# Block 1's row statistics taken from VectorE to ScalarE and GpSimd, and its normalization placed behind the last copies of block 0

## The chip, the cores and the metric

The kernel runs on one core of one Trainium2 chip. A core has a matrix engine (TensorE, PE in the profile, with its weight loads as PEld), VectorE (DVE), ScalarE (ACT), GpSimd (POOL) and SyncE (SP), which issues most of the DMA transfers. Each engine works through its own list of instructions in order, and an instruction can wait for semaphores that other engines or DMA transfers raise. The metric is the device time of one execution in microseconds (us); smaller is better. Three runs of the kernel before took 1155.17, 1156.48 and 1157.27 us.

## The reference

The reference applies two layers of two parts each to an input of 2048 rows by 512 columns: a long convolution per column (an S4 state space model whose 2048 coefficients are made from A, B, C and dt), and a gated feed-forward net. Each part works on the normalized rows and is added to its input.

```python
def _layernorm(x, axis=-1, eps=1e-5):
    m = jnp.mean(x, axis=axis, keepdims=True)
    v = jnp.var(x, axis=axis, keepdims=True)
    return (x - m) / jnp.sqrt(v + eps)
...
        P = jnp.exp(logdA[:, :, None] * l[None, None, :])
        K = jnp.einsum("dn,dnl,dn->dl", Cc, P, dB).real
...
        Yf = Uf * Kf[None, :, :, :]
...
        y = (lambda x, *d: x.transpose(*d))(y, 0, 2, 1) + u * Dskip[None, None, :]
...
        g = _silu(x @ w_gate)
        u = x @ w_up
        return (g * u) @ w_down
...
    x = A_u
    x = x + _A_ref(_layernorm(x, axis=-1), ...)
    x = x + _B_ref(_layernorm(x, axis=-1), ...)
    x = x + _A_ref(_layernorm(x, axis=-1), ...)
    x = x + _B_ref(_layernorm(x, axis=-1), ...)
```

Uf and Kf are the transforms of the padded rows and coefficients, y the transform of Yf back. The change concerns one of the normalizations: that of rows 512 to 1023 (block 1) ahead of the first convolution. For each row it needs the mean m and 1/sqrt(v + eps); the normalized row is then x times a scale plus a bias of -m times the scale.

## The kernel before

The rows are taken in four blocks of 512, each held as four tiles of 128 rows by 512 columns. The convolution is done with matrix products against constant tables: `direct` (line 290) makes the spectra of a block, four frequency groups q for each of two halves h of the columns, and the copies at line 299 carry each of these eight results from PSUM (pf) to SBUF (u), from where SyncE stores it to DRAM (udr, line 300). Blocks 0 and 1 have their first-layer spectra made early, while the convolution's coefficients are still being built; the later part of the kernel reads them back.

The coefficients are built in eight chunks of 64 columns. For each chunk VectorE builds a table g (`gen_g`, lines 458 to 486) and tables of exponentials times cosines and sines (`gen_e`, lines 444 to 451; line 451 is the last of them). ScalarE makes the exponentials (`gen_exp`, lines 420, 424 and 436), their squares mu (`upper`, line 430), and the cosines and sines (`gen_trig`, lines 406 to 411). TensorE sums over the states in `lags` (lines 496 and 497, into pk), ScalarE copies the result to ks (line 507), SyncE stores it and loads it back in another order as kt (`spread`, lines 514 and 516), VectorE adds the skip term to kt (line 503), TensorE makes kt's spectra pw (line 531), ScalarE copies these (lines 554 and 559), and VectorE adds two parts (line 563). The last doubling of g is added by an accumulating DMA of 1 MB that GpSimd issues (line 476). In between, the largest norms of the weights are summed: GpSimd loads rows of w_down, w_gate and w_up (line 327), ScalarE squares them (line 333), and TensorE sums the squares (nrm, line 336).

From chunk 0's products on, the order of this work is written as a table of times (`plan`), sorted, and issued in that order; the lines that the change touches stand just ahead of that table and are issued in the order in which they are written. For ScalarE, VectorE, TensorE and GpSimd no scheduler reorders them; SyncE's queue is ordered by a scheduler up to the table.

Block 1's rows are the tile x1 (loaded at line 126). Its statistics are taken by `stats` (line 196), the same function as for block 0: VectorE runs one BN_STATS and one BN_AGGR for each of the four row tiles (lines 203 and 204), adds eps (line 205), GpSimd raises to the power -1/2 (line 206), and VectorE makes the bias (line 209). ScalarE applies scale and bias at line 998, between the exponentials of chunk 1 and the last three copies of line 299, and SyncE stores the normalized rows to DRAM (ndr, line 1001). `second` (line 304) loads halves of them back (n1, line 309) for block 1's own `direct`, whose eight parts are spread over the table. The tile kt2, which takes both kt copies, uses x1's buffer.

A second function, `row_stats` (line 212), takes statistics with ScalarE in later stages: an Identity pass with a running sum gives the mean (line 219), a Square pass with a running sum the variance (line 221), a small step adds eps (line 222), GpSimd takes the power (line 223), and VectorE makes the bias (line 224).

Of the kernel before, what the change touches and what calls it, by code (L numbers as in the profile page):

```python
# [13 lines left out]
BF16 = mybir.dt.bfloat16  # L14
I32 = mybir.dt.int32
AF = mybir.ActivationFunctionType
OP = mybir.AluOpType
# [4 lines left out]
L, D, F = 2048, 512, 1376  # L22
P = 128
# [4 lines left out]
HD = D // 2  # L28
# [46 lines left out]
def kernel(ctx, tc, x, a_re, a_im, b_re, b_im, c_re, c_im, log_dt, d_skip,  # L75
                           w_gate, w_up, w_down, c_ef, c_ei, c_ek, c_am, c_eh, c_eih, out):
    nc = tc.nc
    V, A, G, PE = nc.vector, nc.scalar, nc.gpsimd, nc.tensor
# [9 lines left out]
    def tl(shape, name, tag, dt=F32):  # L88
        return sb.tile(shape, dt, name=name, tag=tag, bufs=BUFS[tag])
# [35 lines left out]
    x1 = tl([P, 4, D], "x1", "xf")  # L125
# [9 lines left out]
    mhalf = sb.tile([P, 4], F32, name="mhalf")  # L135
    G.memset(mhalf, -0.5)
    epst = sb.tile([P, 2], F32, name="epst")
# [13 lines left out]
    ndr = dram.tile([2, 2, P, 2, HD], F32, name="ndr")  # L151
# [44 lines left out]
    def stats(src, rows, scale, tag="stats", then=None):  # L196

        st = tl([P, 4, 6], "st", tag)
        mv = tl([P, 4, 2], "mv", tag)
        rs = tl([P, 8], "rs", tag)  # L200
        nb = rs[:, 4:]
        for r in range(rows):
            V.bn_stats(st[:, r], src[:, r])
            V.bn_aggr(mv[:, r], st[:, r])
        V.tensor_scalar(rs[:, :rows], mv[:, :rows, 1], EPS, 1.0 / scale ** 2, OP.add, OP.mult)
        G.tensor_tensor(rs[:, :rows], rs[:, :rows], mhalf[:, :rows], OP.pow)
        if then:
            then()
        V.scalar_tensor_tensor(nb[:, :rows], mv[:, :rows, 0], -1.0, rs[:, :rows], OP.mult, OP.mult)
        return rs, nb  # L210
# [174 lines left out]
    def gen_turns(ch, ts):  # L385

        re, im, mu, xz, mz = ts
        cs = slice(ch * DC, (ch + 1) * DC)
        V.tensor_tensor(xz[:, 1].bitcast(I32), th[:, cs].bitcast(I32).unsqueeze(1).to_broadcast([P, 5, DC]),
                        am.unsqueeze(2).to_broadcast([P, 5, DC]), OP.logical_shift_left)  # L390
        yield
        tu = im[:, 33:65].bitcast(I32)
        V.tensor_tensor(tu[:, 0:2], th32[:, cs].bitcast(I32).unsqueeze(1).to_broadcast([P, 2, DC]),
                        am[:, 0:2].unsqueeze(2).to_broadcast([P, 2, DC]), OP.logical_shift_left)
        yield
        for n in (2, 4, 8, 16):
            V.tensor_tensor(tu[:, n:2 * n], tu[:, 0:n], tu[:, n - 1:n].to_broadcast([P, n, DC]), OP.add)
            yield
        G.memset(im[:, 32], 0.0)
        yield  # L400

    def gen_trig(ts):


        re, im, mu, xz, mz = ts
        A.activation(xz[:, 2], xz[:, 1].bitcast(I32), AF.Sin, scale=-TWO_PI / TURN)
        for c, s in ((xz[:, 0], xz[:, 1]), (re[:, 33:65], im[:, 33:65])):
            turns = s.bitcast(I32)
            A.activation(c, turns, AF.Abs)
            A.activation(s, turns, AF.Sin, scale=TWO_PI / TURN)  # L410
            A.activation(c, c, AF.Sin, scale=-TWO_PI / TURN, bias=hpi)
            yield
# [26 lines left out]
    def gen_e(ts):  # L439


        re, im, mu = ts[:3]
        half = [[t.rearrange("p a (g h d) -> p a g h d", g=4, h=2)[:, :, :, o] for t in (re, mu)] for o in range(2)]
        V.tensor_tensor(im[:, :32], im[:, 64:32:-1], re[:, :32], OP.mult)
        yield
        V.tensor_tensor(re[:, :32], re[:, 64:32:-1], re[:, :32], OP.mult)
        yield
        V.scalar_tensor_tensor(im[:, 33:64], im[:, 31:0:-1], -1.0, mu[:, 1:], OP.mult, OP.mult)
        yield
        for r, u in half:  # L450
            V.tensor_tensor(r[:, 33:64], r[:, 31:0:-1], u[:, 1:], OP.mult)
            yield
# [176 lines left out]
    def take(it, n):  # L629
        for _ in range(n):  # L630
            next(it, None)
# [321 lines left out]
    with tc.manual_schedule(engines={mybir.EngineType.Activation, mybir.EngineType.DVE, mybir.EngineType.PE, mybir.EngineType.Pool}):  # L953
# [3 lines left out]
        def turns():  # L957
            V.tensor_tensor(rho, rho, dt, OP.mult)
            take(first, 1)
            take(ex, 14)  # L960
            take(others, 1)
            take(first, 1)
            take(gen_turns(0, ts[0]), 7)
        ft = tl([P, 2, 2, D], "ft", "ga")
        first, others = turn_units(ft, 0, DC), turn_units(ft, DC, D)
        stats_x = stats(xe, 4, 1.0, then=lambda: (turns(), take(others, 1)))
# [10 lines left out]
        gg = gen_g(0, ts[0], gs[0])  # L977
        ge, tn = gen_e(ts[0]), gen_turns(1, ts[1])
# [2 lines left out]
        upper(ts[0])  # L981
        take(fw[0], 1)
        take(tn, 7)
        stats_x = stats(x1, 4, 1.0, then=lambda: (take(gg, 1), take(ge, 1)))
        tr = gen_trig(ts[1])
        take(tr, 1)
        take(fw[1], 1)
# [6 lines left out]
        take(ex, 14)  # L994
        take(fw[4], 1)
        take(ex, 13)
        for c in range(4):
            A.activation(x1[:, c], x1[:, c], AF.Identity, scale=stats_x[0][:, c:c + 1], bias=stats_x[1][:, c:c + 1])
        for h in range(2):
            for cp in range(2):  # L1000
                nc.sync.dma_start(ndr[h, cp], x1[:, 2 * cp:2 * cp + 2, h * HD:(h + 1) * HD])
        for g in (gg, ge, gg, ge, ge):
            take(g, 1)
        for f in fw[5:]:
            take(f, 1)
        kt2 = tl([P, 2, 4, 16, 16], "kt2", "xf")
        sec = [(h, q) for h in range(2) for q in QORD]
        plan = []
# [87 lines left out]
        for i in range(NCH - 1):  # L1096
# [6 lines left out]
            for k, t0, t1, t2, t3 in ((0, -13.0, 0.25, 13.9, 22.3), (1, 0.3, 14.5, 17.45, 22.9),  # L1103
                                      (2, 15.0, 26.5, 28.05, 36.0)):
                n = ((3, 3, 0), (3, 3, 0), (3, 3, 0), (3, 2, 0), (3, 2, 0), (3, 3, 0), (3, 3, 3))[i][k]
                if i == NCH - 2 and k == 2:
                    t0, t1, t2, t3 = 15.0, 20.0, 24.0, 27.0
# [11 lines left out]
        c, kts, tail = NCH - 1, (kt2[:, 0], kt2[:, 1]), {}  # L1119
# [151 lines left out]
```

## Time and profile before

| | |
|---|---|
| median of three runs | 1156.48 us (1155.17 to 1157.27) |
| the profiled execution's own time | 1156.48 us |
| its span in the profile | 1154.7 us |
| granted TensorE clock, mean | 0.991 |
| BN_STATS of x1 | first at 28.29 us, four of 0.67 us |
| scale and bias of x1 (line 998) | 49.62 us, four passes, 2.92 us |
| first stores of ndr (line 1001) | 51.15 us |
| block 1's first product (pf<-n, line 296) | 64.19 us |

The profile is one execution on the chip. A row of the timeline gives its start from the span's start, the time it took, the engine, the line, the operation, and what it writes and reads; x4 after it means that four such instructions follow each other. In square brackets stand the idle time of the engine ahead of it and what ended that time. In groups by line the figures behind the bar are the total, the mean of one in ns, and the idle time. A row of the DMA view ends with the size of one transfer and the median time from issue to landing. In a table by stretch the busy time of each engine is given; instructions of one engine can overlap by a little, so that rows of the timeline start about 0.1 us before the one ahead has ended.

### The profile page before, as it was taken

How to read it: one execution, taken by the hardware profiler on the slowest of the kernel's cores; microseconds unless marked ns; L12 is line 12 of the kernel's file. 1: busy time of each engine (PE TensorE's matmuls, PEld its weight loads, DVE VectorE, ACT ScalarE, POOL GpSimd, SP SyncE). 2: the span in 40 equal slices, each digit the busy share in tenths (PEclk: the TensorE clock that was granted, in tenths of full speed). 3: DMA queues.
4: the chain of work that ended last, by engine and by line, in shares of the span. 5: the costliest groups of instructions: out<-in, count | busy, mean ns of one | idle time of the engine just before them, and what ended most of it. 6: DMA issues, size and time to landing. Idle time of an engine off the chain costs nothing.

```text
span 1154.7 us, 24400 instructions
## 1 busy us (share of the span) xinstructions
PE 1100.2 (95%) x9942; PEld 877.6 (76%) x9942; DVE 998.7 (86%) x1585; ACT 599.1 (52%) x1198; POOL 109.5 (9%) x163
## 2 busy tenths in 40 slices
PE   2989999998889999999999999999999999999998
PEld 1878888887776868686868687877778686876875
DVE  8999999988889899999899999989994999973211
ACT  6989889734553453567453534555434352334211
POOL 0112222210000010011010001111000100000000
PEclk9989999999899999999999999999999999999999
DMA  5367777867473446332253454343444145312000
GB/s 209 128 165 165 161 185 170 193 186 244 164 240 110 129 139 207 111 102 74 89 153 124 133 156 150 107 120 105 147 121 140 50 130 160 97 37 48 14 24 19
DMA packets 127314, 150.38 MB, mean 130 GB/s; under 512 B 50897, under 2 KB 75985, under 8 KB 127202
## 3 DMA queue, kind: packets, MB, share of 16 engines
q1 hardware_dynamic: 115298, 123.32, 34.9%
q0 software_dynamic: 11904, 25.50, 9.5%
q8 instruction: 78, 1.28, 0.5%
q14 instruction: 34, 0.28, 0.1%
HBM read 98.70 MB, written 33.82 MB: 115 GB/s over the span
## 4 chain that ended last, share of the span: by engine, by line
PE 35%; DVE 23%; issue 8%; DMA 5%; ACT 3%; SPq 1%; POOL 1%; DVEq 0%; ACTq 0%; POOLq 0%
PE pgu L911 6%; PE pgu L912 6%; PE pgu L914 6%; PE py L926 4%; PE py L927 3%; PE py L928 3%; DVE t L776 3%; DVE yk L779 3%; PE pi L798 2%; PE pf L280 2%; DMA w<-wdr 2%; DVE yk L776 2%; DVE z L228 2%; DVE sg L918 1%; DMA mix<-nn 1%
## 5 line engine op out<-in xcount | busy, mean ns | idle before, releaser
L911 PE MATMUL pgu<-mix,wsl 128*128 128x256 f16 x1280 | 299.0, 273 | 4.3 <-DVE sg L918 3.3
L912 PE MATMUL pgu<-mix,wsl 128*128 128x256 f16 x1280 | 298.6, 273 | 0.0
L914 PE MATMUL pgu<-mix,wsl 128*128 128x256 f16 x1280 | 195.7, 273 | 0.0
L912 PEld LDWEIGHTS <-wsl 128*128 128x128 f16 x1280 | 125.4, 98 | 21.2 <-issue 4.8
L926 PE MATMUL py<-wsl,hh 128*128 128x512 f16 (+1 forms) x352 | 133.4, 379 | 6.1 <-DVE xg L931 4.5
L911 PEld LDWEIGHTS <-wsl 128*128 128x128 f16 x1280 | 125.3, 98 | 16.1
L914 PEld LDWEIGHTS <-wsl 128*128 128x128 f16 x1280 | 125.4, 98 | 14.8
L928 PE MATMUL py<-wsl,hl 128*128 128x512 f16 (+1 forms) x352 | 133.4, 379 | 0.8 <-DVE hl L920 0.8
L776 DVE TENSOR_TENSOR t<-uu,w 128x1024 f32<-128x1024 f32 x96 | 116.9, 1217 | 6.6 <-DMA w<-wdr 6.4
L917 ACT ACTIVATE sg<-pgu,sc 128x512 f32<-128x512 f32 x80 | 54.6, 682 | 130.0 <-PE pgu L914 126.8
L927 PE MATMUL py<-wsl,hh 128*128 128x512 f16 x320 | 121.3, 379 | 0.0
L779 DVE TENSOR_TENSOR yk<-yk,t 128x1024 f32<-128x1024 f32 x96 | 116.8, 1216 | 0.2
L918 DVE SCALAR_TENSOR_TENSOR sg<-pgu,sc,sg 128x512 f32<-128x512 f32 x80 | 59.6, 745 | 52.0 <-ACT sg L917 51.8
L531 PE MATMUL pw<-kt,ek 128*128 128x256 f32 (+1 forms) x384 | 91.8, 376 | 0.0
L919 ACT ACTIVATE hh<-sg 128x512 f16<-128x512 f32 x80 | 50.1, 627 | 76.3 <-DVE sg L918 76.3
L531 PEld LDWEIGHTS pw<-kt,ek 128*128 128x128 f32 x384 | 73.3, 195 | 8.6
L798 PE MATMUL pi<-yl,mix 128*128 128x256 f16 x576 | 78.9, 272 | 0.6 <-DVE yl L228 0.3
L280 PE MATMUL pf<-z,eh 128*128 128x256 f16 x576 | 74.9, 273 | 0.8 <-DVE z L228 0.6
L776 DVE TENSOR_TENSOR yk<-u,w0r 128x1024 f32<-128x1024 f32 x56 | 68.2, 1217 | 0.8 <-ACT u L282 0.8
L920 DVE TENSOR_TENSOR hl<-sg,hh 128x512 f16<-128x512 f32 x80 | 54.8, 685 | 15.5 <-ACT hh L919 15.5
L496 PE MATMUL pk<-re,g 128*32 128x64 f32 x1024 | 65.1, 317 | 2.4 <-DMA g<-g 2.4
L927 PEld LDWEIGHTS <-hh 128*128 128x128 f16 (+1 forms) x352 | 34.5, 98 | 42.7 <-issue 7.3
(238 smaller groups left out, 2164.3 us busy)
## 6 DMA issues: line engine op xcount, KB each, us to landing
uu<-udr SPq DMA_DIRECT2D x96, 256.0 KB, 3.0
w<-wdr SPq DMA_DIRECT2D x96, 256.0 KB, 2.7
udr<-u POOLq DMA_DIRECT2D x32, 256.0 KB, 2.6
g<-g POOLq DMA_DIRECT2D x6, 1024.0 KB, 9.0
udr<-u SPq DMA_DIRECT2D x16, 256.0 KB, 3.5
n<-xdr SPq DMA_DIRECT2D x4, 1024.0 KB, 5.6
kdr<-ks SPq DMA_DIRECT2D x6, 512.0 KB, 2.9
kt<-kdr SPq DMA_DIRECT2D x24, 128.0 KB, 3.1
```

What stands on the lines that cost most here:

```text
L280: PE.matmul(pf[:, o], lhsT=e, rhs=m, start=k == 0, stop=k == len(terms) - 1)
L531: PE.matmul(pw[:, i], lhsT=e, rhs=kt[:, :, c + 4 * k0:4 * k1:4, :].rearrange("p g k d -> p k g d"), start=c == 0, stop=c == 3)
L776: V.tensor_tensor(t, uu.unsqueeze(2).to_broadcast([P, NQ, 2, 2, DC]), w.unsqueeze(3).to_broadcast([P, NQ, 2, 2, DC]), OP.mult)
L779: V.tensor_tensor(yk, yk, t, OP.add)
L798: PE.matmul(pi[:, o], lhsT=e, rhs=m, start=k == 0, stop=k == len(terms) - 1)
L911: PE.matmul(o, lhsT=wgu(wi, k, 0)[:, fs], rhs=nh[:, k], start=k == 0, stop=False)
L912: PE.matmul(o, lhsT=wgu(wi, k, 1)[:, fs], rhs=nh[:, k], start=False, stop=False)
L914: PE.matmul(o, lhsT=wgu(wi, k, 0)[:, fs], rhs=nlo[:, k], start=False, stop=k == 3)
L918: V.scalar_tensor_tensor(sg, pgu[:, 1], sc6[:, 4:5], sg, OP.mult, OP.mult)
L926: PE.matmul(py[:, r], lhsT=hh[:n, f, rc], rhs=wd(f, 0)[:n], start=f == 0, stop=False)
L927: PE.matmul(py[:, r], lhsT=hh[:n, f, rc], rhs=wd(f, 1)[:n], start=False, stop=False)
L928: PE.matmul(py[:, r], lhsT=hl[:n, f, rc], rhs=wd(f, 0)[:n], start=False, stop=f == FT - 1)
```

## The change

VectorE's statistics of x1 are removed. In their place, at the point where the normalization stood, ScalarE makes two passes per row tile that only matter for their running sums: an Identity pass with the scale -1/512, whose sum is the negative mean, and a Square pass of the row with that as bias, whose sum is 512 times the variance. A small ScalarE step divides by 512 and adds eps. GpSimd takes the power -1/2 and multiplies it with the negative mean, which gives the bias. The four normalizing passes and the four stores of ndr now stand behind the last three copies of block 0 (`fw[5:]`). The two steps of `gen_g` and `gen_e` that ran between the statistics stay where they were.

```diff
@@ -981,7 +981,8 @@
         upper(ts[0])
         take(fw[0], 1)
         take(tn, 7)
-        stats_x = stats(x1, 4, 1.0, then=lambda: (take(gg, 1), take(ge, 1)))
+        take(gg, 1)
+        take(ge, 1)
         tr = gen_trig(ts[1])
         take(tr, 1)
         take(fw[1], 1)
@@ -994,15 +995,23 @@
         take(ex, 14)
         take(fw[4], 1)
         take(ex, 13)
+        mv, rs = tl([P, 4, 2], "mv", "stats"), tl([P, 8], "rs", "stats")
         for c in range(4):
-            A.activation(x1[:, c], x1[:, c], AF.Identity, scale=stats_x[0][:, c:c + 1], bias=stats_x[1][:, c:c + 1])
-        for h in range(2):
-            for cp in range(2):
-                nc.sync.dma_start(ndr[h, cp], x1[:, 2 * cp:2 * cp + 2, h * HD:(h + 1) * HD])
+            A.activation(tl([P, D], "junk", "t1", BF16), x1[:, c], AF.Identity, scale=-1.0 / D, accum_out=mv[:, c, 0:1])
+        for c in range(4):
+            A.activation(tl([P, D], "junk", "t1", BF16), x1[:, c], AF.Square, bias=mv[:, c, 0:1], accum_out=mv[:, c, 1:2])
+        A.activation(mv[:, :, 1], mv[:, :, 1], AF.Identity, scale=1.0 / D, bias=epst[:, 0:1])
+        G.tensor_tensor(rs[:, :4], mv[:, :, 1], mhalf, OP.pow)
+        G.tensor_tensor(rs[:, 4:], mv[:, :, 0], rs[:, :4], OP.mult)
         for g in (gg, ge, gg, ge, ge):
             take(g, 1)
         for f in fw[5:]:
             take(f, 1)
+        for c in range(4):
+            A.activation(x1[:, c], x1[:, c], AF.Identity, scale=rs[:, c:c + 1], bias=rs[:, 4 + c:5 + c])
+        for h in range(2):
+            for cp in range(2):
+                nc.sync.dma_start(ndr[h, cp], x1[:, 2 * cp:2 * cp + 2, h * HD:(h + 1) * HD])
         kt2 = tl([P, 2, 4, 16, 16], "kt2", "xf")
         sec = [(h, q) for h in range(2) for q in QORD]
         plan = []
```

On ScalarE, in the place between the end of chunk 1's exponentials (re) and its squares mu, the order of before and now (x is block 1's tile, pf the products of block 0, u their copies, mv the sums):

```order
 L436 ACTIVATE re<-re 128x8x64
 L436 ACTIVATE re<-re 128x4x64
-L998 ACTIVATE x_89<-x_89,rs 128x512 x4
+L1000 ACTIVATE junk,mv<-x_89 128x512 x4
+L1002 ACTIVATE junk,mv<-x_89,mv 128x512 x4
+L1003 ACTIVATE mv<-mv,epst 128x4
 L299 ACTIVATE u<-pf 128x2x4x64 x3
+L1011 ACTIVATE x_89<-x_89,rs 128x512 x4
 L430 ACTIVATE mu<-re 128x1984
```

Nine instructions stand ahead of the copies where four stood, and four behind them.

On GpSimd, in the place between the clearing of chunk 1's first columns and the first loads of weights for the norms (st), the order of before and now:

```order
 L422 MEMSET re 128x64
 L399 MEMSET im 128x64 x2
-L206 TENSOR_TENSOR rs<-rs,mhalf 128x4
 L422 MEMSET re 128x64
+L1004 TENSOR_TENSOR rs<-mv,mhalf 128x4
+L1005 TENSOR_TENSOR rs<-mv,rs 128x4
 L317 MEMSET cmx 128x2
 L327 DMA st<-in_B_w_down_dram 128x512 x6
```

The power stands behind the clearing and with the product ahead of the loads; the loads are what they were.

On SyncE, in the place of block 0's stores (udr), the stores of block 1's rows (ndr) and the loads back (n), before:

```order
L300 DMA udr_114<-u 128x512 x5
L1001 DMA ndr<-x_89 256x1x256 x4
L300 DMA udr_114<-u 128x512 x2
L309 DMA n_440<-ndr 128x512
L309 DMA n_442<-ndr 128x512
L300 DMA udr_114<-u 128x512
L514 DMA kdr<-ks 128x1024
```

and now:

```order
L300 DMA udr_114<-u 128x512 x8
L1014 DMA ndr<-x_89 256x1x256 x4
L309 DMA n_447<-ndr 128x512
L309 DMA n_449<-ndr 128x512
L514 DMA kdr<-ks 128x1024
```

All of block 0's stores now go ahead of block 1's. On VectorE the ten instructions of lines 203 to 205 and 209 are gone, and nothing else has moved; TensorE's order is the same.

## The prediction

> **What bounds the kernel now.** I read the page's first part, then the table of busy time by stretch around the edited lines, then VectorE's waits behind them, and at last the timeline between 28 and 86 us, engine by engine. In the table the columns after the stretch and its length are PE, PEld, DVE, ACT and POOL busy us, the granted TensorE clock, the DMA share and GB/s.
>
> ```profile
> PE 1100.2 (95%) x9942; PEld 877.6 (76%) x9942; DVE 998.7 (86%) x1585; ACT 599.1 (52%) x1198; POOL 109.5 (9%) x163
> 32.00:72.00 40.00, 36.51 (x385) 31.83 (x385) 39.38 (x45) 37.18 (x90) 4.67 (x10) 0.99 0.47 159
> 86.00:240.00 154.00, 151.52 (x1956) 133.66 (x1949) 151.53 (x185) 130.91 (x285) 38.26 (x56) 1.00 0.73 175
> DVE wsl L669 <- ACT wsl L664: 4.8, 1, 4.8
> DVE cmx L339 <- PE nrm L336: 2.1, 1, 2.1
> DVE wo L563 <- ACT w0r L559: 0.7, 1, 0.7
> ```
>
> The last three rows are all that VectorE waits for between 86 and 300 us (total, times, longest). Over the whole span PE is the busiest engine, but the edit lies where VectorE is full: 39.38 of 40 us, 151.53 of 154. What decides is at what time VectorE leaves 86 us. ScalarE is nearly as full in the stretch where the new work goes (37.18 of 40), so the relief of one engine is the load of the next. Behind 86 us I carry a shift of VectorE to the end in full: its three waits end on ScalarE and PE steps that work on what VectorE wrote, so they move along. If they did not, they could swallow it; that is the low side of the range.
>
> **What leaves VectorE.** Four pairs of statistics, their scaling and the product that makes the bias.
>
> ```profile
> L203 DVE BATCH_NORM_STATS2 st<-x 128x6 f32<-128x512 f32 x4 | 2.7, 666 | 0.0
> L204 DVE BATCH_NORM_AGGREGATE mv<-st 128x2 f32<-128x6 f32 x4 | 0.7, 182 | 0.2
> 29.56 1.06 ACT L436 ACTIVATE re<-re 128x512 f32<-128x512 f32 x2
> 32.02 2.29 DVE L444 TENSOR_TENSOR im<-im,re 128x2048 f32<-128x2048 f32 x1
> 57.02 2.31 DVE L444 TENSOR_TENSOR im<-im,re 128x2048 f32<-128x2048 f32 x1
> ```
>
> That is 2.7 + 0.7 = 3.4 us and two small ones. Not all of it comes back: the next large step, L444, multiplies exponentials that ScalarE finishes with L436 at 29.56 + 1.06 = 30.62 us. So L444 moves from 32.02 to 30.65 at best: a gain of 1.4 us. From there VectorE runs on its own up to 57 us, where the second L444 would start at some 55.7 instead of 57.02 (its neighbour writes the buffer that the block-0 matmuls read up to about 55.3). I take 1.3 us.
>
> **What ScalarE gains.** First its own rows of before; then the price of the new passes, from the same passes in later stages (L219 and L221 are the Identity and Square passes with a sum, four rows in a row of the first).
>
> ```profile
> 49.62 2.92 ACT L998 ACTIVATE x<-x,rs 128x512 f32<-128x512 f32 x4
> 52.44 1.06 ACT L299 ACTIVATE u<-pf 128x512 f32<-128x512 f32 x2
> 55.32 0.67 ACT L299 ACTIVATE u<-pf 128x512 f32<-128x512 f32 x1 [1.83 <-PE pf L296]
> 55.83 2.17 ACT L430 ACTIVATE mu<-re 128x1984 f32<-128x1984 f32 x1
> 63.67 1.02 ACT L507 ACTIVATE ks<-pk 128x1024 f32<-128x1024 f32 x1 [0.71 <-PE pk L497]
> 884.00 0.63 ACT L219 ACTIVATE junk<-n 128x512 bf16<-128x512 f32 x1 [3.64 <-DMA n<-xdr]
> 886.46 0.71 ACT L221 ACTIVATE junk<-n,mv 128x512 bf16<-128x512 f32 x1
> 890.37 0.28 ACT L222 ACTIVATE mv<-mv,epst 128x4 f32<-128x4 f32 x1
> ```
>
> In ScalarE's order eight passes and a small one now stand ahead of the three copies at 52.44 and 55.32, and the normalization behind them. Four Identity passes take 886.46 - 884.00 = 2.46 us, four Squares 4 x 0.71 = 2.84, the small one 0.3: 5.6 us, from 49.62 to 55.2. The copies take 1.06 + (55.83 - 55.32) = 1.6 and no longer wait for PE, whose last block-0 product is there at 55.3: the 1.83 us of waiting are used. They end at 56.8.
>
> **What GpSimd gains.** A power, as before but later, and a product; both now stand ahead of L317 and of the first loads of w_down, L327, which before were issued at 33.05.
>
> ```profile
> 31.92 1.05 POOL L206 TENSOR_TENSOR rs<-rs,mhalf 128x4 f32<-128x4 f32 x1 [19.18 <-DVE rs L205]
> 262.07 0.31 POOL L503 TENSOR_TENSOR kt<-kt,tdk 1x64 f32<-1x64 f32 x1 [17.29 <-ACT kt L525]
> 473.22 1.22 DVE L779 TENSOR_TENSOR yk<-yk,t 128x1024 f32<-128x1024 f32 x1
> 473.49 1.83 POOL L223 TENSOR_TENSOR rs<-mv,mhalf 128x4 f32<-128x4 f32 x1
> 579.43 4.02 POOL L223 TENSOR_TENSOR rs<-mv,mhalf 128x2 f32<-128x2 f32 x1 [31.81 <-ACT mv L222]
> 33.05 1.82 POOL L327 DMA_DIRECT2D st<-in_B_w_down_dram  x3
> st<-in_B_w_down_dram POOLq DMA_DIRECT2D x6, 256.0 KB, 4.1
> ```
>
> At 31.92 the power took 1.05 us beside short VectorE steps. At 473.49 it started inside a VectorE product with both inputs in SBUF and ended 0.88 us after that product (473.22 + 1.22 = 474.44, and 475.32); at 579.43 it took 4.02. So I read: such a GpSimd step stands still until the VectorE product that is running ends. Here the power starts at 55.4, beside two short products (as at 31.92), and ends at 56.4. The new product then starts inside L444, which runs from 55.7 to 58.0. No row shows a multiplication of this shape on GpSimd; the nearest, the addition, took 0.31. Between an end at 56.8 (no wait) and 60.2 (55.4 + 4.02 for the power, 0.3 for the product and a VectorE step in between) I take 58.5: L444's end, 0.3, and a short VectorE step in between, since 473.49 is the row that it is nearest to.
>
> The Trainium skill ("SBUF — State Buffer", section "Who interferes with whom") says that a VectorE instruction with two SBUF inputs and a GpSimd instruction that reads SBUF block each other, the first to issue holding the port for its whole length. By that the product ends at 58.3 to 58.5; without the rule it would be 56.8 and the sum 0.6 us. Its other half, that the power should hold up VectorE, is not borne out: L444 began 0.1 us into the power of 31.92 and took 2.29, as its other run took 2.31.
>
> So the four normalizing passes run from 58.5 (pitch 0.7, as 49.62 to 52.44) to 61.3, where L430 starts: 61.3 - 55.83 = 5.5 us late. The wait of 0.71 ahead of L507 takes some up: L507 and the Squares L333 behind it are 4.8 us late.
>
> The moved loads of w_down cost nothing: issued over 1.82 us from 58.6 and landed 4.1 us later, at 62.7 to 64.5, they meet Squares that begin behind L430, at 61.3 + 2.1 = 63.4, one after the other. That cover is thin; a landing 1 us later costs nearly 1 us.
>
> SyncE's queue changes too: all eight stores of block 0's spectra now go ahead of the four stores of the normalized rows, then the two loads back.
>
> ```profile
> ndr<-x SPq DMA_DIRECT2D x4, 256.0 KB, 2.6
> n<-ndr SPq DMA_DIRECT2D x2, 256.0 KB, 4.6
> 64.19 0.59 PE L296 MATMUL pf<-n,ef 128*128 128x256 f32 x2
> 71.30 1.62 PE L336 MATMUL nrm<-sq,onesb 128*128 128x512 bf16 x3 [3.49 <-ACT sq L333]
> 73.61 1.22 PE L531 MATMUL pw<-kt,ef 128*128 128x256 f32 x2 [0.68 <-DVE kt L503]
> 81.53 1.46 PE L531 MATMUL pw<-kt,ek 128*128 128x256 f32 x6
> 67.39 1.76 SPq L516 DMA_DIRECT2D kt<-kdr  x4
> kt<-kdr SPq DMA_DIRECT2D x4, 128.0 KB, 3.0
> 72.75 1.26 POOL L476 DMA_DIRECT2D g<-g  x1 [8.90 <-DVE im L393]
> 73.35 0.20 DVE L503 TENSOR_TENSOR kt<-kt,tdk 1x64 f32<-1x64 f32 x1
> 84.01 0.95 ACT L554 ACTIVATE wo<-pw 128x384 f32<-128x384 f32 x2
> 84.82 0.40 ACT L559 ACTIVATE w0r<-pw 128x256 f32<-128x256 f32 x1
> 86.00 0.97 DVE L563 TENSOR_TENSOR wo<-pw,wo 128x768 f32<-128x768 f32 x1
> 71.30:78.10 6.80, 6.12 (x14) 3.81 (x14) 6.70 (x9) 3.62 (x4) 3.06 (x5) 0.50 0.56 96
> ```
>
> The last store issues at 61.3 and lands 2.6 later, and the loads land up to 4.6 after that (a pair later in the kernel; no row is nearer), at some 68.5: the product pf<-n starts there instead of at 64.19. Its 3.6 us (64.19 to the idle time of 3.49 ahead of 71.30) end at 72.1, ahead of the sums nrm, which wait for the late Squares until 76.1 anyway. Nothing is lost there. The stores also free the buffer that kt takes over; they have read it by 64, long before kt's loads.
>
> **The sum.** Two paths lead back to VectorE.
> - By the copy of kt: L507 4.8 us late makes SyncE's four loads 4.8 late. In before the first landed at 67.39 + 3.0 = 70.4 and L503 read it at 73.35: 3.0 of slack. L503 is 1.8 us late.
> - By PE: nrm 4.8 late ends at 72.92 + 4.8 = 77.7, so pw starts there instead of at 73.61: 4.1 late. In before pw ended at 82.99 and L554 began at 84.01 (1.0 of slack); L559 ended at 85.22 and L563 began at 86.00 (0.8). L563 is 4.1 - 1.0 - 0.8 = 2.3 us late.
>
> The 1.3 us gained before are lost in both waits. The larger counts: 2.3. To it I add 0.2, since the loads of kt now run beside the accumulating 1 MB of L476, which in before began behind them. The profiled execution took 1156.48 us (span 1154.7), which is also the median of the runs shown. 1156.48 + 2.5 = 1159.0 us, 0.2% slower. A difference under 0.2% (2.3 us) I call no change, about what a measurement of this kernel can tell; the forecast lies at that edge.
>
> **Rivals.**
> 1. GpSimd does not wait: the normalization starts at 56.8, 1.7 us earlier. Then L507 is 3.1 late, L503 0.1, L563 0.6: 1157.1. For it: 31.92 us, where the power took 1.05 with L444 beside most of it. Against: 473.49.
> 2. GpSimd loses its turn again and again, as at 579.43. The normalization then starts at 60.2, 1.7 us later than I took: 1160.7. For it: the short VectorE steps that follow each other at 58; against: at 31.92, in the same place of block 0's chain, the power got its turn at once.
> 3. The loads of kt suffer from L476. Beside software DMA the loads of 256 KB above took 4.6 us, where the stores of as much took 2.6. If kt's need 1.6 more than 3.0, L503 is 3.4 late: 1159.9.
> 4. TensorE's clock: after 3.49 us without matmuls it was 0.50 from 71.30 to 78.10. pw ran 78.10 - 73.61 = 4.5 us of it; with full clock it is half of that, 2.2 us, shorter, so only kt's path counts: 1158.5. The idle stretch after the change, 72.1 to 76.1, is longer than before's, so I expect 0.50 again. By the Trainium skill ("TensorE: Matmul & The Clock Gate", Part 1) an idle window of about 3.4 us halves the clock and the windows run freely; the trace agrees, with 3.49 us.
> 5. Not slower, the other side: ScalarE's delay at L507 stays under 2.5 us (the point that decides: there both paths just keep up), since the passes overlap better than I add them. As far as it stays under that, VectorE keeps its gain, up to 1.3 us: 1155.2. For it: both paths have their slack. Against: 5.6 + 1.6 + 2.8 us of ScalarE's own work from 49.62 already end at 59.6, 3.8 late.
>
> **How the numbers follow.** Chances: my forecast 0.36 (a little over half of it above 2.3 us), rival 1 0.18, 2 0.17, 3 0.16, 4 0.08, 5 0.05. Slower by over 0.2%: 0.17 + 0.16 + 0.22 = 0.55. Within: 0.18 + 0.08 + 0.05 + 0.14, less 0.03 for a measurement that falls below: 0.42. Faster: 0.03. The range: 1155.8 (between rivals 5 and 1) to 1162.7 (rival 2, with the loads of w_down 1 us late and kt's 1 us slower as well).
>
> **What would show it.** L1003 ends near 55.4 us; L1005 ends near 58.5 and at L444's end; L1011 starts there, waiting for GpSimd; L430 at 61.3; L503 waits for kt, at about 75; L563 waits for L559, at about 88.3; from there every VectorE row stands about 2.4 us later than before. It is wrong if L1011 starts at 56.8, if L503 and L563 show no idle time before them, or if the shift at 86 us is not the shift at the end.

## The result and the profile after

The changed kernel takes 1165.42 us (median of four, 1163.90 to 1168.07), the kernel before 1155.95 beside it: a ratio of 1.0083, with an interval of 1.0071 to 1.0095. It is slower, as forecast, but by 9.5 us instead of 2.5. The first profiled execution is the slowest of the four (1168.07 us, span 1166.2); a second, at 1162.12, comes with the experiments.

First the table by stretch of the kernel after, in the columns of before.

```profile
32.00:72.00 40.00, 33.03 (x364) 28.41 (x363) 39.17 (x46) 36.62 (x80) 8.96 (x12) 0.91 0.40 141
86.00:240.00 154.00, 153.23 (x2008) 136.12 (x2007) 150.06 (x184) 134.75 (x286) 38.23 (x56) 0.99 0.72 167
71.30:78.10 6.80, 6.35 (x19) 4.41 (x17) 0.52 (x2) 6.55 (x31) 2.25 (x4) 0.70 0.98 209
```

VectorE is as full as before up to 72 us and from 86 on. In the stretch between, the third row, it is busy for 0.52 us instead of 6.70, and the DMA share is 0.98 instead of 0.56. Of its waits between 28 and 300 us (total, times, longest) two are not in before:

```profile
DVE kt L503 <- DMA kt<-kdr: 8.8, 1, 8.8
DVE im L444 <- ACT re L436: 2.1, 1, 2.1
```

L444's 2.1 us is the time that the statistics left free, until the exponentials are there. The wait that costs is the other, 8.8 us for the loads of kt. The timeline says how it comes about; GpSimd, ScalarE, VectorE, PE and SyncE, one below the other.

```profile
55.23 4.07 POOL L1004 TENSOR_TENSOR rs<-mv,mhalf 128x4 f32<-128x4 f32 x1 [43.60 <-ACT mv L1003]
59.38 0.47 POOL L1005 TENSOR_TENSOR rs<-mv,rs 128x4 f32<-128x4 f32 x1
71.17 1.26 POOL L476 DMA_DIRECT2D g<-g  x1 [3.85 <-DVE im L393]
54.85 0.30 ACT L1003 ACTIVATE mv<-mv,epst 128x4 f32<-128x4 f32 x1
59.89 3.10 ACT L1011 ACTIVATE x<-x,rs 128x512 f32<-128x512 f32 x4 [3.10 <-POOL cmx L317]
62.89 1.84 ACT L430 ACTIVATE mu<-re 128x1984 f32<-128x1984 f32 x1
69.29 1.00 ACT L507 ACTIVATE ks<-pk 128x1024 f32<-128x1024 f32 x1
30.52 2.29 DVE L444 TENSOR_TENSOR im<-im,re 128x2048 f32<-128x2048 f32 x1 [2.10 <-ACT re L436]
80.65 0.21 DVE L503 TENSOR_TENSOR kt<-kt,tdk 1x64 f32<-1x64 f32 x1 [8.80 <-DMA kt<-kdr]
94.98 0.97 DVE L563 TENSOR_TENSOR wo<-pw,wo 128x768 f32<-128x768 f32 x1 [1.63 <-ACT w0r L559]
84.05 1.19 PE L531 MATMUL pw<-kt,ef 128*128 128x256 f32 x2 [5.73 <-DMA kt<-kdr]
73.28 4.49 SPq L516 DMA_DIRECT2D kt<-kdr  x4
```

The power took 4.07 us, so the normalization began at 59.9, L430 at 62.9 (7.1 late) and the copy to ks, L507, at 69.3 (5.6 late). SyncE issued the four loads of kt from 73.28 on, and took 4.49 us for it where it had taken 1.76. That is 2.1 us behind the issue of L476, the accumulating DMA, which GpSimd issued at 71.17; in before the loads went out 5.4 us ahead of it (67.39 and 72.75). Two rows of after's DMA view, for what was issued from 60 to 80 us:

```profile
g<-g POOLq DMA_DIRECT2D x1, 1024.0 KB, 9.0
kt<-kdr SPq DMA_DIRECT2D x4, 128.0 KB, 7.4
```

The queues of this execution from 73.3 to 78 us (packets, MB, share of the time of 16 engines; packets can overlap, so a share can pass 100%):

```profile
q0 software_dynamic: 208, 0.85, 108.0%
```

and those of the second profile from 75 to 78 us:

```profile
q0 software_dynamic: 129, 0.53, 87.9%
q1 hardware_dynamic: 128, 0.13, 15.7%
```

A load of kt takes 7.4 us instead of 3.0. The software queue (q0) carries the transfers that GpSimd issues, the hardware queue (q1) SyncE's. In the first execution q1 has no row: for 4.7 us L476's packets move, 208 of 4.1 KB each, and of the loads issued from 73.28 on not one packet. In the second the queues take turns, 129 packets of 4.1 KB to 128 of 1.0 KB, so that 3 us carry no more than one load of kt. The Trainium skill ("DMA: Bandwidth & Descriptors", section "Queues, rings and completion order") says that each DMA engine takes turns between the queues that have work, a packet at a time; the equal counts of the second profile agree with it, and why nothing of kt moved in the first is not shown. In both, L503 could start only when L476 was ending or done: at 80.65 and 78.60 us.

PE waited for the last of the four loads, until 84.05. By then it had also met three loads of w_down, issued at 77.15, whose 0.79 MB move between 80 and 84 us. Of the 9.0 us by which L563 is late (94.98 against 86.00), 7.3 are L503's (80.65 against 73.35) and the rest PE's path.

Behind L563 nothing more is lost: instruction by instruction, VectorE is 9.0 us later than in before at 100 us, 8.9 at 200 and 8.5 at 600. In this execution 2.8 more come at 900, which the second profile does not show; e6, below, which has no part of the change, shows 3.0 there. Their cause is not known.

### The profile page after: what moved, and what is told of

The parts are those of the page before. It is cut to its first block, busy times and chain, and to the rows that moved or that the text cites. A ratio compares the mean times of both kernels' runs of the same rounds, so it can differ in the third digit from the quotient of the medians.

```text
span 1166.2 us, 24409 instructions
## 1 busy us (share of the span) xinstructions
PE 1101.7 (94%) x9942; PEld 877.5 (75%) x9942; DVE 995.9 (85%) x1575; ACT 603.7 (52%) x1215; POOL 112.4 (10%) x164
## 4 chain that ended last, share of the span: by engine, by line
DVE 30%; PE 28%; issue 8%; DMA 5%; ACT 3%; SPq 1%; POOL 1%; DVEq 0%; ACTq 0%; POOLq 0%
DVE t L776 5%; PE pgu L911 5%; PE pgu L912 5%; PE pgu L914 4%; DVE yk L779 4%; PE py L926 3%; PE py L927 3%; PE py L928 3%; DVE z L228 3%; DVE yk L776 3%; DVE sg L918 2%; PE pi L798 2%; DMA w<-wdr 2%; DVE hl L920 2%; PE pf L280 2%
```

## The experiments

My theory from this point (A): the time goes where the loads of kt meet the traffic of L476, and everything ahead of that only sets whether they meet. Its rivals: that GpSimd's wait is itself carried to the end (B), that ScalarE's longer work is, or that the place of the normalization and its stores costs the time. In every run the kernel before was timed on the same chip.

**The move alone, and the statistics alone.** The two halves of the change.

The first diff is e4 against before, the second e5 against after; the four stores move with the passes.

```diff
-        for c in range(4):
-            A.activation(x1[:, c], x1[:, c], AF.Identity, scale=stats_x[0][:, c:c + 1], bias=stats_x[1][:, c:c + 1])
...
         for f in fw[5:]:
             take(f, 1)
+        for c in range(4):
+            A.activation(x1[:, c], x1[:, c], AF.Identity, scale=stats_x[0][:, c:c + 1], bias=stats_x[1][:, c:c + 1])
...
```

```diff
+        for c in range(4):
+            A.activation(x1[:, c], x1[:, c], AF.Identity, scale=rs[:, c:c + 1], bias=rs[:, 4 + c:5 + c])
...
         for f in fw[5:]:
             take(f, 1)
-        for c in range(4):
-            A.activation(x1[:, c], x1[:, c], AF.Identity, scale=rs[:, c:c + 1], bias=rs[:, 4 + c:5 + c])
...
```

> The kernel before, with only the second half of the change: the four normalizing passes and the four stores behind the last three copies of block 0; the statistics stay on VectorE. By my steps: the copies end at 55.9, where they ended, since they wait for PE either way; the normalization runs from 55.9 to 58.7, L430 starts 2.9 us late, L507 2.2 late, the loads of kt land at 72.6 at the latest, still ahead of L503, nrm ends at 75.1 and pw starts 1.5 late, which the 1.8 us of room behind it take up. Theory A: no loads slower than 3.3 us, the total within 1 us of before. If the place of the stores (behind all of block 0's, beside the loads of kt) is itself what costs: n lands late, pf<-n late, the total 1159 or more.

> The kernel after, with only the first half of the change: the statistics by ScalarE and GpSimd stay, the four normalizing passes and the four stores go back ahead of the last three copies of block 0. By my steps: GpSimd is ready at 57.7 to 59.8 as in the runs so far, nothing covers its wait now, so the passes run to 60.8 to 62.9, the copies to 62.5 to 64.6, L430 starts there (6.7 to 8.8 us late) and L507 is 6 to 8 us late. Theory A (the loads of kt meet L476's traffic, issued at 71.2): the loads go out at 73.4 or later, all of them take 6.5 us or more, L563 is 8 to 11 us late and the total 1163 to 1167. Rival (the place of the normalization is what made the change slow): 1158 or less.

The move alone: 1156.41 us against 1155.40, ratio 1.0008 (0.9999 to 1.0018). The normalization and L563 in its timeline:

```profile
55.60 3.24 ACT L1002 ACTIVATE x<-x,rs 128x512 f32<-128x512 f32 x4
85.69 0.95 DVE L563 TENSOR_TENSOR wo<-pw,wo 128x768 f32<-128x768 f32 x1
```

The power and the normalization in the timeline of the statistics alone:

```profile
55.26 4.06 POOL L1004 TENSOR_TENSOR rs<-mv,mhalf 128x4 f32<-128x4 f32 x1 [43.60 <-ACT mv L1003]
59.88 3.10 ACT L1007 ACTIVATE x<-x,rs 128x512 f32<-128x512 f32 x4 [4.70 <-POOL cmx L317]
```

The move costs nothing that can be measured: L563 stands where it stood (85.69, 86.00 in before). The statistics alone cost all of it, 1166.07 us against 1155.57, 1.0100 (1.0083 to 1.0116): nothing covers GpSimd's wait of 4.70 us, and L503 waits 10.3 us for kt. The place of the normalization, as a cause, is out.

**Lateness alone, in the kernel before.** No part of the change, only idle passes on ScalarE ahead of chunk 0's L507: twelve in e6, six in e11.

```diff
             def copy():
+                for _ in range(12 if c == 0 else 0):
+                    A.activation(tl([P, D], "junk", "t1", BF16), w0[:, 0], AF.Identity)
                 box["ks"] = spread_in(box["pk"])
```

> The kernel before, with nothing of the change: twelve idle passes of 512 elements on ScalarE ahead of chunk 0's L507, each 0.55 us, so that ks is 6.0 to 6.6 us late (69.7 to 70.3 instead of 63.7). VectorE keeps its statistics; GpSimd's power is where it was; L476 is issued at 72.8 as in before. Theory A (lateness of ks makes the loads of kt meet L476): they are issued from 73.4 on and take 6 to 8 us each, L503 runs at 79 to 81, the total is 7 to 9 us above before, 1162.5 to 1164.5. Rival (the lateness is only carried): the loads land in 3 us, L503 at 76.8 is 3.5 late, PE's path 4 late, the total 1159 to 1160.

> The kernel before with six idle passes ahead of chunk 0's L507 where the run above had twelve: 3.2 us late instead of 5.8. Theory A (a threshold at the moment at which the loads of kt meet L476's traffic): L507 runs at 66.3 to 66.9, the loads of kt go out from 69.9 to 71.7, before L476 is issued at 72.5, and take 3 us; L503 is 0 to 1 us late, PE's path 0.5 to 2 late, the total 1156 to 1157.5, that is 0.5 to 2 us above before. Rival (the time lost grows evenly with the lateness): half of what twelve passes cost, 4.5 us, 1160.

Twelve passes: 1164.69 us against 1155.57, ratio 1.0083 (1.0068 to 1.0098). Six: 1155.85 against 1155.41, 1.0003 (0.9994 to 1.0012). ScalarE's timeline with twelve:

```profile
63.17 6.35 ACT L1057 ACTIVATE junk<-w 128x512 bf16<-128x512 f32 x12 [0.52 <-PE nrm L336]
69.43 1.00 ACT L507 ACTIVATE ks<-pk 128x1024 f32<-128x1024 f32 x1
```

and its loads of kt in the DMA view:

```profile
kt<-kdr SPq DMA_DIRECT2D x4, 128.0 KB, 8.3
```

The same two with six:

```profile
66.37 1.00 ACT L507 ACTIVATE ks<-pk 128x1024 f32<-128x1024 f32 x1
```

```profile
kt<-kdr SPq DMA_DIRECT2D x4, 128.0 KB, 3.0
```

L507 2.7 us late costs nothing, 5.8 us late costs 9.1. It is a threshold, not a slope, and the kernel before has it too: nothing of GpSimd or of the statistics is needed. One detail of the expectation is off: with twelve passes L503 ran at 76.0, since the first load of kt came through; PE waited for a later one (4.4 us), and L563 was 7.2 us late, 2.7 of them L503's.

**The collision taken away.** The kernel after, with chunk 1's L476 issued behind the last load of kt (e2). In e10 the first three loads of w_down also stand ahead of GpSimd's power.

```diff
+                if ch == 1:
+                    G.tensor_tensor(dmy[96:97], kt2[96:97, 0, 0, 1], kt2[96:97, 0, 0, 1], OP.add)
                 G.dma_start(g[:, :, 16:32].rearrange("p i b d -> p i (b d)"), tmp.rearrange("p i b d -> p i (b d)"),
                             accum_op=OP.add)
```

> The kernel after, in which chunk 1's accumulating DMA (L476) is issued only when the last load of kt has landed: GpSimd first adds 16 elements of that load's rows into a tile that nobody reads. All lateness on ScalarE and GpSimd stays (L507 at 69.3). Theory A (the loads of kt are slow because of L476): they are issued from 73.3 to 74.5 and land in 2.6 to 3.3 us, by 77.7; L503 runs at 76 to 77.9 instead of 80.65, L563 3 to 5 us late instead of 9, the total is 1159 to 1161. Rival (they are slow by their own lateness, behind the store of ks or other loads, and L476 only runs beside them): 7 us each again, L503 at 80.5, the total 1165.

> The kernel after with all eight passes on ScalarE, chunk 1's accumulating DMA (L476) issued only behind the last load of kt, and the first three loads of w_down ahead of GpSimd's power. Theory A: the loads of kt take 3 us whenever they go out. If GpSimd is quick (1.0 us of power and a product that ends with VectorE's L444, at 57.8), L507 runs at 67.5, L503 at 74 to 75; if the power loses its turn (4 us), L507 at 69, L503 at 76. The total is 1155.5 to 1159.5; the loads of w_down ahead make at most 1 us of difference to the run with the guard alone (1158.7). Rival (the loads of w_down behind the power cost more than that, by the Squares that wait for them): 1155 or less.

e2: 1158.72 us against 1155.40, ratio 1.0029 (1.0018 to 1.0039), a little less than I expected, since GpSimd's power was quick in it. e10: 1159.74 us against 1155.41, 1.0050 (1.0030 to 1.0070), 0.2 us above my range; one of its four times is 1164.32. The timeline of e10: the power, the copy, and VectorE's two steps.

```profile
55.34 4.07 POOL L1008 TENSOR_TENSOR rs<-mv,mhalf 128x4 f32<-128x4 f32 x1 [32.45 <-ACT mv L1006]
69.41 1.00 ACT L510 ACTIVATE ks<-pk 128x1024 f32<-128x1024 f32 x1
75.82 0.21 DVE L506 TENSOR_TENSOR kt<-kt,tdk 1x64 f32<-1x64 f32 x1 [3.88 <-DMA kt<-kdr]
88.48 0.95 DVE L566 TENSOR_TENSOR wo<-pw,wo 128x768 f32<-128x768 f32 x1
```

Its ScalarE and GpSimd are as late as in after (the copy, L507 in after and L510 here, at 69.29 and 69.41, the power 4.07 us in both), only the loads are quick again (3.0 us each, from 2.9 to 3.1), and the last of VectorE's two steps falls from 94.98 to 88.48: the collision is 6.5 us of the 9.0. What stays is 88.48 - 86.00 = 2.5 us. In e2 the power took 1.01 us, the copy ran at 67.55 and VectorE's last step at 87.71. In the times, 6.6 to 9.5 us above before in the two measurements of after fall to 3.3 and 4.3. The guard holds back the three loads of w_down behind L476 as well (issued at 78.86 in e2); in after these move only from 80 us on, so the lateness of the first load of kt is L476's, and that of the last may be theirs in part. In e10 the Squares began at 64.73, in after at 64.64: the loads of w_down ahead make no difference.

**The kernel after once more.**

> The kernel after once more, unchanged, since the profile so far is that of its slowest execution. Theory A: whether GpSimd's power takes 4.07 us or 1.0 decides only how many of kt's loads meet L476's traffic (issued at 71.2). At 4.07 L507 runs at 69.3, all four loads take 6.5 us or more, L563 is 8.5 to 9.5 us late and the total 1163.5 to 1166; the shift at 86 us is then that at 600 us to within 1 us, and what the first profile has beyond that (11.4 at the end) is its own. At 1.0 L507 runs at 67.5 to 68.2, only the later of the four loads are slow, L563 is 5 to 6 late, the total 1160 to 1163. Rival (the slow loads are a feature of that one execution): L503 at 75 to 76, the total 1159 to 1160.

1162.62 us (six runs, 1161.14 to 1165.21) against 1156.06, ratio 1.0065 (1.0053 to 1.0077). The profiled execution took 1162.12; its timeline:

```profile
55.18 1.01 POOL L1004 TENSOR_TENSOR rs<-mv,mhalf 128x4 f32<-128x4 f32 x1 [43.44 <-ACT mv L1003]
56.27 1.84 POOL L1005 TENSOR_TENSOR rs<-mv,rs 128x4 f32<-128x4 f32 x1
67.92 1.00 ACT L507 ACTIVATE ks<-pk 128x1024 f32<-128x1024 f32 x1
78.60 0.21 DVE L503 TENSOR_TENSOR kt<-kt,tdk 1x64 f32<-1x64 f32 x1 [6.41 <-DMA kt<-kdr]
92.15 0.99 DVE L563 TENSOR_TENSOR wo<-pw,wo 128x768 f32<-128x768 f32 x1 [0.85 <-ACT w0r L559]
```

The slow loads are no feature of one execution. All four take 7.2 to 8.1 us here too, which I had expected of the later ones only. L563 is 6.2 us late, and VectorE is 5.6 to 5.7 late from 500 us to the end. Against e2, with the copy at nearly the same time (67.92 and 67.55), the collision is 92.15 - 87.71 = 4.4 us.

**GpSimd out of the way.** In e1 the normalizing passes use a constant tile, and the power stands behind the first loads of w_down.

```diff
-            A.activation(x1[:, c], x1[:, c], AF.Identity, scale=rs[:, c:c + 1], bias=rs[:, 4 + c:5 + c])
+            A.activation(x1[:, c], x1[:, c], AF.Identity, scale=fix[:, c:c + 1], bias=fix[:, 4 + c:5 + c])
-        G.tensor_tensor(rs[:, :4], mv[:, :, 1], mhalf, OP.pow)
...
+        at(0.15, lambda: G.tensor_tensor(rs[:, :4], mv[:, :, 1], mhalf, OP.pow))
```

> The kernel after, with nothing on ScalarE waiting for GpSimd: the four normalizing passes take a scale and bias of 1 from a constant tile (so the normalization of block 1 is left out of the result, not of the time), and the power and its product stand behind the first three loads of w_down, which are issued at 33 us as in before. The eight passes stay on ScalarE. Theory A (what costs the most is that the loads of kt meet the traffic of L476): the copies end at 56.8, the normalization runs 56.8 to 59.6, L430 starts at 59.7 (+3.9 on before), L507 at 66.9 (+3.2), the loads of kt are issued at 70.6 to 72, ahead of L476's traffic (its issue of 71.2 to 72.4), and land in some 3 us each; L503 runs at 73.6 to 74.2, L563 is 1 to 3 us late, the total is 1157 to 1159. Theory B (GpSimd's wait of 4.07 us is itself carried to the end, one for one): L1011 starts 3.1 us earlier than in after (56.8 against 59.9), the total is 9.5 - 3.1 = 6.4 us above before, 1162.

1153.76 us against 1155.40, ratio 0.9989 (0.9980 to 0.9999). The copy, the loads of kt, L476 and L563 (L478 and L565 here) in its timeline:

```profile
66.53 1.00 ACT L509 ACTIVATE ks<-pk 128x1024 f32<-128x1024 f32 x1
70.25 1.76 SPq L518 DMA_DIRECT2D kt<-kdr  x4
71.20 1.26 POOL L478 DMA_DIRECT2D g<-g  x1 [6.58 <-DVE im L395]
86.23 0.96 DVE L565 TENSOR_TENSOR wo<-pw,wo 128x768 f32<-128x768 f32 x1 [0.63 <-ACT w0r L561]
```

B would have made it 1162, so GpSimd's wait isn't carried one for one. The loads go out 0.95 us ahead of L476's issue and take 3.0; with all eight passes on ScalarE, the time is not above before's. It came out better than A's 1157 to 1159: L563 was 0.2 us late where I had written 1 to 3. VectorE gains 2 to 3 us more on before's profile behind 240 us, far from the edit. About 1 us of that is the profile of before: its execution, at 1156.48, is 1.1 us above the median beside e1, and e11 and e8 (below), which have no part of the change, gain 1.0 and 1.4 us on it between 100 and 600 us. The rest I can't explain.

**One input for VectorE's product.** In e3 chunk 1's L444 reads one input of the same size. What it would have written is set to zero by GpSimd, at 12 us.

```diff
-        V.tensor_tensor(im[:, :32], im[:, 64:32:-1], re[:, :32], OP.mult)
+        if ts is one_in:
+            V.tensor_reduce(red, im[:, 33:65], axis=AX.X, op=OP.max)
+        else:
+            V.tensor_tensor(im[:, :32], im[:, 64:32:-1], re[:, :32], OP.mult)
...
+        G.memset(ts[1][1][:, :32], 0.0)
```

> The kernel after, with chunk 1's L444 (VectorE, 2.3 us, two inputs in SBUF) replaced by a maximum along the rows of one of its inputs, so that VectorE reads one input of the same size for about as long; that product is left out of the result. If GpSimd's power is held up by VectorE's instructions with two SBUF inputs: it starts at 55.2 and takes 1 to 1.5 us, the product ends at 57, L1011 starts at 57, L507 is 3 to 3.6 us late, the loads of kt go out ahead of L476's traffic and the total is 1157 to 1160. If the power is slow by itself, or beside any VectorE work: 4 us again, L1011 at 59.8, the total 1165.

Its timeline, on GpSimd, VectorE and SyncE:

```profile
55.02 1.16 POOL L1010 TENSOR_TENSOR rs<-mv,mhalf 128x4 f32<-128x4 f32 x1 [40.97 <-ACT mv L1009]
56.26 0.20 POOL L1011 TENSOR_TENSOR rs<-mv,rs 128x4 f32<-128x4 f32 x1
55.22 2.30 DVE L446 TENSOR_REDUCE red<-im 128x32 f32<-128x2048 f32 x1
70.90 1.77 SPq L520 DMA_DIRECT2D kt<-kdr  x4
70.96 1.26 POOL L480 DMA_DIRECT2D g<-g  x1 [5.78 <-DVE im L394]
91.73 0.99 DVE L567 TENSOR_TENSOR wo<-pw,wo 128x768 f32<-128x768 f32 x1 [5.47 <-ACT w0r L563]
```

and the last line of what the trace says of the tile kt:

```profile
DMA to landing us min/median/max: 2.8/4.9/7.8
```

GpSimd's product takes 0.20 us inside a one-input reduction of 2.30; beside the two-input L444 it took 1.84 in the second profile of after. By the Trainium skill ("SBUF — State Buffer", section "Who interferes with whom") a VectorE instruction with one SBUF input does not compete with GpSimd; this row agrees. It is a single row, and in e9, below, the product also took 0.20 us where it began as one two-input instruction of VectorE ended and the next began. But the total is 1161.77 us (1.0051, 1.0034 to 1.0068), not 1157 to 1160: SyncE's loads went out at 70.90, 0.06 us ahead of L476's issue, and of the four some landed in 2.8 us and some in 7.8. Compared with e1, 0.65 us in SyncE's issue and 0.24 in L476's make 5.5 us at L563 (91.73 and 86.23). The ten times of this kernel reach from 1154.36 to 1164.20, as one expects of a kernel that stands on the threshold.

**Two tries for a faster kernel.** e7 keeps the change, puts the loads of w_down ahead of the power, chunk 0's copy to ks ahead of the small sines, and pw ahead of nrm. e8 has the two moves of the table without the change.

```diff
-            at(t + 7.1, copy)
+            at(t + (7.1 if c else 0.3), copy)
...
-            for q0, ats in list(enumerate(((t + 17.5, t + 25.2, n + 2.1, n + 7.5),
+            for q0, ats in list(enumerate(((t + (17.5 if c else 17.4), t + 25.2, n + 2.1, n + 7.5),
```

> The kernel after with the whole change in it, and three places of the order moved: the first three loads of w_down ahead of GpSimd's power, chunk 0's copy to ks (L507) ahead of the cosines and sines of the small table and its table load (3.2 us on ScalarE), and chunk 0's products pw ahead of the second three sums nrm. Theory A: the copy then runs between 63.7 and 66.6 (the later, if GpSimd's power takes 4 us), the loads of kt go out from 67.4 to 70.3, ahead of L476's traffic, and land in 3 us; L503 runs at 71.9 to 73.4; VectorE keeps 0 to 1.5 us of what it gained; the total is 1153 to 1156, not slower than before. Rival (ScalarE's longer work is carried anyway, by the Squares and the sines behind the copy): L563 is 2 us late or more, the total 1157.5 or more.

> The kernel before with the same two moves of the order (the copy to ks ahead of the small sines, pw ahead of nrm) and nothing of the change. In before L507 waits for the products pk (0.71 us), so it cannot run earlier than 63.6: L503 stays at 73.3, behind VectorE's own work, and pw, which waits for L503, starts at 73.6 as before. The total is within 1 us of before. If it is more than 1.5 us below before, the moves themselves are a gain, and what the kernel above shows is not the change's.

e8 is 1155.32 us against 1155.57 (1.0001, 0.9992 to 1.0010), as expected. e7 is 1165.11 us, 1.0075 (1.0059 to 1.0090): my expectation failed. Its timeline on GpSimd and SyncE:

```profile
64.73 1.67 POOL L327 DMA_DIRECT2D st<-in_B_w_down_dram  x3 [6.00 <-ACT sq L333]
63.37 3.08 SPq L309 DMA_DIRECT2D n<-ndr  x2
66.50 0.43 SPq L514 DMA_DIRECT2D kdr<-ks  x1
73.31 4.43 SPq L516 DMA_DIRECT2D kt<-kdr  x4
```

and the store of ks in its DMA view:

```profile
kdr<-ks SPq DMA_DIRECT2D x1, 512.0 KB, 6.7
```

The copy was early, at 65.25 us, and its store went out at 66.50, but right behind three loads of w_down and the two loads of n: it took 6.7 us where it took 2.6 in before, and the loads of kt went out at 73.31, as late as in after. It looks like the same crowding, one transfer earlier; no run takes these transfers apart.

In e9 VectorE takes the statistics of two of the four row tiles and ScalarE those of the other two; the loads of w_down stand ahead of the power.

```diff
+        for c in range(2):
+            V.bn_stats(st[:, c], x1[:, c])
+            V.bn_aggr(mv[:, c], st[:, c])
+        V.tensor_scalar(mv[:, :2, 0], mv[:, :2, 0], -1.0, None, OP.mult)
+        V.tensor_scalar(mv[:, :2, 1], mv[:, :2, 1], EPS, None, OP.add)
         take(gg, 1)
         take(ge, 1)
...
-        for c in range(4):
+        for c in range(2, 4):
             A.activation(tl([P, D], "junk", "t1", BF16), x1[:, c], AF.Identity, scale=-1.0 / D, accum_out=mv[:, c, 0:1])
```

> The kernel after with the work shared: VectorE takes the statistics of row tiles 0 and 1 (it sits idle until 30.6 us ahead of L444 anyway, so its gain of 1.4 to 1.5 us should stay), ScalarE those of 2 and 3 (four passes instead of eight, 49.4 to 52.4), and the first three loads of w_down stand ahead of GpSimd's power. The power then starts at 52.4 and has until 55.9, when the last copy of block 0 ends, so its wait is covered even if it takes 3 us; the normalization runs from 55.9 to 58.9 as in the run with the move alone, L507 at 65.5, the loads of kt go out at 69.2 to 71, ahead of L476's traffic (its issue of 71.2 to 72.4). Theory A: they land in 3 us, L503 runs at 72.2 (1.1 earlier than in before), L563 at 84.9 to 86, the total is 1153.5 to 1155.5, 0 to 2 us below before. Rival (any of ScalarE's passes are carried to the end, 2.7 us of them): 1157 to 1159.

The power, the loads of kt and L563 in its timeline:

```profile
52.57 1.28 POOL L1011 TENSOR_TENSOR rs<-mv,mhalf 128x4 f32<-128x4 f32 x1 [29.76 <-ACT mv L1009]
68.57 1.76 SPq L516 DMA_DIRECT2D kt<-kdr  x4
84.49 0.95 DVE L563 TENSOR_TENSOR wo<-pw,wo 128x768 f32<-128x768 f32 x1
```

GpSimd's wait is covered, the loads go out 2.7 us ahead of L476, VectorE waits for none of kt's loads and L563 is 1.5 us earlier than in before. The rival (2.7 us of ScalarE's passes carried) is out. The time is 1155.69 us against 1155.41, 1.0003 (0.9994 to 1.0013), just above the 1153.5 to 1155.5 that I expected: the loss is gone, and no gain can be measured. The profiled execution kept the 1.5 us to its end (2.2 at 1140 us), but this compares two single executions: e9's, at 1154.36, is 1.3 us below its median, and before's, at 1156.48, 1.1 above the one beside it. That the 1.5 us are worth anything in the time is not shown. No complete version that beats before was found.

## Why the prediction was right in direction and wrong in size

- **What leaves VectorE** (1.4 us, 1.3 taken): right. L444 runs at 30.52, and VectorE is 1.5 to 1.6 us ahead until 73 us.
- **What ScalarE gains** (passes to 55.2): right. L1003 ends at 54.85 + 0.30 = 55.15.
- **What GpSimd gains** (ready at 58.5): both cases that I had weighed occur. In five executions (e1, e2, e3, e7, e12) the power took 1.01 to 1.18 us, and a product that began beside L444 ended with it or a short step behind it: in the second profile of after at 56.27 + 1.84 = 58.1. In three (after, e5, e10) the power took 4.06 or 4.07 us, rival 2's price, and the product ended at 59.9. In after it outlasted L444 (57.77) by 1.5 us, so that my reading, a step that stands still until the running product ends, does not cover it. What decides between the cases is not shown: the power began 0.17 to 0.24 us ahead of chunk 1's L444 in the three, and 0.19 to 0.59 ahead of it, or of the instruction in its place, in the five.
- **L430 at 61.3, L507 4.8 us late**: 61.3 and 4.3 in the second profile, 62.9 and 5.6 in the first.
- **Loads of w_down, SyncE's order**: both cost nothing, as said. The products pf<-n began at 70.7 instead of 68.5, and nrm behind them still waited 0.17 us for the Squares. The 4.6 us for the loads of n were not from the nearest row; before's own pair, in the DMA view from 30 to 66 us, took 3.5:

```profile
n<-ndr SPq DMA_DIRECT2D x2, 256.0 KB, 3.5
```

- **Two paths back to VectorE, 1.8 and 2.3 us**: the size is right, but the path that I let count is not the one that did. With the collision taken away L503 is 1.7 and 2.5 us late (e2, e10), and L563 the same 1.7 and 2.5 without any wait of its own: kt's path alone. PE's path was shorter than I had it, since pw ran at a clock of 1.00 (76.8 to 84 us in e2, 78 to 85.5 in e10) and not at the 0.50 that I expected again. That is rival 4, and that 2.3 lies between 1.7 and 2.5 is luck. In e2, with the copy 3.9 us late, kt's path is 0.8 us longer than 3.9 - 3.0, since the store of ks took 3.7 us instead of 2.6.
- **The loads of kt beside L476, 0.2 us**: here it failed. The term measures 4.4 us (second profile of after against e2) to 6.5 (first against e10). I had seen the loads move beside L476 and had rival 3 for it, but took their price, 1.6 us, from loads of 256 KB that met software packets of 0.6 KB (788 packets, 0.49 MB, from 165 to 172 us). L476's packets have 4.1 KB, and 1 MB of them took 9 us; the loads take turns with them or do not move at all until it is nearly done. The row to read was its landing: 8.9 us long in before, and issued at 71.17 after the change, it ends at 80, and L503 got its load at 80.65.
- **The shift carried to the end**: right within 1 us up to 800 us. 9.0 us at 86 us and 8.5 at 600; 6.2 and 5.6 in the second profile; 9.5 and 6.6 between the medians.

Without the failed term the sum is +2.3 us. e2 and e10, the change without the collision, stand 1.7 and 2.5 us late at L563; their times are 3.3 and 4.3 us above before, 1.6 and 1.8 more. The rows are those of single executions: the profiled ones of e2 and e10 took 1157.78 and 1158.21 us, 0.9 and 1.5 below their medians, and that of before is 1.1 above the median beside them. That is as much as the gap; why executions of one kernel differ by this is not known.

## What to carry to other kernels

Where an edit delays a small transfer, look not only at how much slack its reader has, but at which large transfer is issued next on another queue: being 2.7 us late cost nothing here, 5.8 us cost 9. For the price take the time until the large transfer lands, not the slowdown between transfers of like size. And a kernel that passes such a point by hundredths of a microsecond, as e3 does, varies from run to run (1154.36 to 1164.20); order the large transfer behind the small one, or keep a margin.

## What the runs showed of the hardware that I had not expected

- Beside an accumulating DMA of 1 MB (9.0 us), four loads of 128 KB on SyncE's queue took 7.4 us (6.6 to 7.5; 7.9 in the second profile) instead of 3.0, and their four issues 4.49 us (3.60) instead of 1.76. In the first execution they moved no packet from 73.3 to 78 us, while the other queue moved 208; in the second the queues moved 128 and 129 in 3 us.
- Behind other transfers a store of 512 KB took 6.7 us instead of 2.6 (e7).
- A GpSimd power of 128x4 elements behind L1003 took 1.01 to 1.18 us in five executions and 4.06 or 4.07 in three. The first is possible beside VectorE's two-input product: 55.30 to 56.48 us in e1, with the product at 55.49, which still took 2.31 us. GpSimd's product behind it, with two inputs, took 0.20 us beside a one-input instruction (e3) and 1.29 to 2.21 where it began beside the two-input one (e1, e2, e7, e12), and ended behind that one's end each time.
